# Order of uppers, loads and the first outer-product step in a retention + two-FFN kernel

## Chip, cores and metric

One core of a Trainium2 chip. The metric is device time in microseconds (us) of one execution. Besides it a profile gives the span, from the first to the last instruction that the profiler recorded.

## What is computed

Three stages, each fed by the one before; inputs are 32-bit floats, the weights arrive as 64-bit floats.

```
# q, k, v: (4, 8, 768, 64); gamma[h] = 1 - 2**(-5 - h); scale = 1/sqrt(64)
state = gamma * state + k[t] (outer) v[t]
y[t]  = scale * q[t] @ state
x = y as (3072 tokens, 512)
h = x @ w_in;  g = max(0.01*h, h);  x = g @ w_out        # 512x2048, 2048x512
h = x @ w2_in; g = h - tanh(h);     out = g @ w2_out
```

## The kernel before

**Attention (functions `a_*`).** 24 steps, one for each of six blocks of 128 positions (`c`) and four pairs of heads (`p`), in chunked form. A step on TensorE: transposes of the keys (`kTp`) and queries (`qTp`), the state's part of `y`, the scores' part of `y`, the state update `u` (not in the last block), and the next step's scores `sc`. ACT scales the keys two steps ahead (`k`) and copies the transposes to SBUF (`kT`, `qT`) and `y` to `x1`; DVE applies decay and mask to the scores (`A`) and updates the state `U`. All engines work in the order in which the program issues.

**Two parts for each matrix operand.** A 32-bit matrix is an upper part (a rounded copy, made by ACT in `upper`) and a lower part (the difference, made by DVE or POOL in `lower`); a product of two matrices takes three matmuls: upper by upper, upper by lower, lower by upper.

**Stream: the first GEMM of FFN1.** For three groups of blocks `sb` (two blocks `c` each) and eight groups `g` of columns of `w_in`, a 2x2 block product is made of seven products P1 to P7 (a Strassen-like scheme) in place of eight, six 128x512 matmuls each. Their results meet in PSUM banks X, Y and Z. `build_wg(g)` makes the operands of a weight set: the sums `s12` and `s34` on DVE, their uppers on ACT and lowers on DVE. `build_xc(sb, part)` makes the seven blocks of activations: B11, B21, T1 in part 0; T2, B22, T3, T4 in part 1. The T blocks are differences made in place by `minus` (T1, T2 on DVE; T3, T4 on POOL), then split into `xch` (upper) and `xcl` (lower). For sb 0 the blocks come from tiles in SBUF, later ones are loaded back by `load_xq`, which shares four buffers with the weights' loads. `stream` is the list of products, sorted by 56·sb + 7·g + an offset of each product (P1 0, P2 1, P5 2, P6 4, P3 5, P7 10, P4 13). After a product `collect` has ACT copy its bank (P1, P5, P6), or DVE add a kept copy to a bank (`add_up`, tile `c`), and one product later ACT rectifies `c` (`rectify`) and SP stores it to `g1s`.

**Background work.** Conversions of weights (`Convert`: ACT takes the absolute value, `cv<-raw`, DVE four steps), weight sets and blocks are generators. `run(queues, us)` takes steps from the first queue that has one ready until the time estimate `us` is used up; a generator that yields None is passed over. In the attention the queues are conversions (`conv`) and `bg`, taking turns as the first; in the stream `bg`, `bx` (loads and blocks), `conv`.

**Outer products and FFN2.** `mm_out1(n)`, n = 0 to 95, multiplies one `g` tile (split by `split_g` into `gh`, `gl`) with rows of `w_out`, 12 matmuls into four banks. FFN2 follows with `mm_l1` and `mm_l2`.

Of the kernel before, what the change touches and what calls it, by code (L numbers as in the profile page):

```python
# [19 lines left out]
P = 128  # L20
NB, NH, NS, ND = 4, 8, 768, 64
DM, DFF = 512, 2048
NC = NS // P
# [46 lines left out]
def kernel(  # L70
# [49 lines left out]
    def run(queues, us):  # L120

        while us > 0:
            for queue in queues:
                cost = next(queue[0], "end") if queue else None
                if cost is not None:
                    break
            if cost is None:
                return 0.0
            if cost == "end":
                queue.popleft()  # L130
            else:
                us -= cost
        return us

    def split(hi, lo, src, eng):

# [3 lines left out]
    def upper(hi, src, scale=None):  # L140
        if scale is None:
            nc.scalar.activation(out=hi, in_=src, func=AF.Copy)  # L142
        else:
            nc.scalar.activation(out=hi, in_=src, func=AF.Copy, scale=scale)
# [108 lines left out]
    def build_wg(g):  # L253
        while g + NG not in UN or g not in UN or len(free) < 10:
            yield None
        a, b = UN.pop(g), UN.pop(g + NG)
        s12, s34 = alloc("s12"), alloc("s34")
        w = {}
        ts = [alloc("wg", F32R) for _ in range(7)]
        for i, (n1, n2) in enumerate((("A11", "A12"), ("S1", "S2"), ("S3", "S4"))):  # L260
            hi, lo = ts[2 * i], ts[2 * i + 1]
            w[n1], w[n2] = (hi[:, :H2], lo[:, :H2]), (hi[:, H2:], lo[:, H2:])
        w["N22"] = ts[6][:, :H2], ts[6][:, H2:]
        upper(ts[0], a)
        nc.vector.tensor_tensor(out=s12[:, :H2], in0=b[:, :H2], in1=b[:, H2:], op=ALU.add)
        yield 0.4
        nc.vector.tensor_tensor(out=s12[:, H2:], in0=s12[:, :H2], in1=a[:, :H2], op=ALU.subtract)
        yield 0.4
        upper(ts[2], s12)
        lower(ts[0], ts[1], a)  # L270
        yield 0.7
        nc.vector.tensor_tensor(out=s34[:, :H2], in0=a[:, :H2], in1=b[:, :H2], op=ALU.subtract)
        yield 0.4
        nc.vector.tensor_tensor(out=s34[:, H2:], in0=a[:, H2:], in1=s12[:, H2:], op=ALU.subtract)
        yield 0.4
        upper(ts[4], s34)
        lower(ts[2], ts[3], s12)
        yield 0.7
        upper(w["N22"][0], b[:, H2:], -1.0)
        lower(ts[4], ts[5], s34)  # L280
        yield 0.7
        lower(*w["N22"], b[:, H2:], -1.0)
        give(a, s12, b, s34)
        WG[g] = w, ts
        yield 0.4
# [18 lines left out]
    def build_xc(sb, part, done=None):  # L304
        while sb not in XQ:
            yield None
        q = XQ[sb]
        old = SPAN * sb - 7
        b11, b12, b21, b22 = q["B11"], q["B12"], q["B21"], q["B22"]

        def minus(eng, out, x, y):
            for kt in range(2):
                eng.tensor_tensor(out=out[kt], in0=x[kt], in1=y[kt], op=ALU.subtract)  # L313


        todo = (("B11", b11, "P1", None), ("B21", b21, "P2", (nc.vector, b11, b12, b11)), ("T1", b11, "P5", None),
                ("T2", b11, "P6", None), ("B22", b22, "P3", (nc.gpsimd, b12, b22, b12)), ("T3", b12, "P7", None),
                ("T4", b21, "P4", None))
        for nm, src, by, nxt in todo[:3] if part == 0 else todo[3:]:
            while sb and now[0] < old + PROD[by][3]:  # L320
                yield None
            if sb:
                for t2 in XC[sb - 1].pop(nm):
                    give(*t2)
            while len(free) < 8:
                yield None
            if nm == "T2":
                minus(nc.vector, b11, b22, b11)
            out = [(alloc("xch", F32R), alloc("xcl", F32R)) for _ in range(2)]
            for kt in range(2):  # L330
                upper(out[kt][0], src[kt])
            yield 0.0
            for kt in range(2):
                lower(*out[kt], src[kt])
                yield 0.7
            XC.setdefault(sb, {})[nm] = out
            if nxt:
                minus(*nxt)
                yield 1.3 if nxt[0] is nc.vector else 0.0
            if nm == "T3":  # L340
                minus(nc.gpsimd, b21, b11, b21)
        if done:
            done()
# [221 lines left out]
    def load_g(n):  # L565
        if n < NT:
            GR[n] = alloc("gr")
            nc.sync.dma_start(out=GR[n], in_=g1s[n // NM, n % NM])


    stream = sorted((SPAN * sb + 7 * g + PROD[nm][3], sb, g, nm)
                    for sb in range(NSB) for g in range(NG) for nm in PROD)
# [63 lines left out]
    conv.extend((conversion(conv2[:W2_EARLY], made(1)),  # L636
                 conversion(conv_out, made(2))))
    bg.extend(build_wg(g) for g in range(2, NG))
    bx = deque()
    for sb in range(1, NSB):  # L640
        bx.extend((load_xq(sb, SPAN * (sb - 1) + 38), build_xc(sb, 0), build_xc(sb, 1)))
    xleft = [(c, p) for c in range(2, NC) for p in range(NPAIR)]
    us = 0.0
    for i, (at_, sb, g, nm) in enumerate(stream):
        an, bn, bk, _ = PROD[nm]
        while g not in WG or bn not in XC.get(sb, {}):
            tick[0] += 1
            run((bg, bx, conv), 0.01)
        product(sb, g, nm)
        now[0] = at_  # L650
        tick[0] += 1
        done, late[:] = late[:], []
        used = collect(sb, g, nm)
        for args in done:
            rectify(*args)
        if sb == NSB - 1 and nm == "P4":
            give(*WG[g][1])
        if xleft:
            c, p = xleft.pop(0)
            t = xw.pop((c, p))  # L660
            nc.sync.dma_start(out=x1s[c, p], in_=t)
            give(t)
        us = run((bg, bx, conv), min(us + SLOT_US - used, SLOT_US))
        if len(stream) - 8 <= i < len(stream) - 8 + G_AHEAD:
            load_g(i - len(stream) + 8)
    for args in late:
        rectify(*args)
    for t2 in XC[NSB - 1].values():
        for t in t2:
            give(*t)  # L670


    xk, xr = {}, {}
    G, H, ACC, Q = {}, {}, {}, {}

    def split_g(n, eng):
        if n < NT:
            G[n] = alloc("gh", F32R), alloc("gl", F32R)
            split(*G[n], GR[n], eng)
            give(GR.pop(n))  # L680

    def mm_out1(n):
        nb, m = divmod(n, NM)
        if m == 0:
            for j in range(4):
                ACC[j] = bank(nb % 2 * 4 + j, f"o1_{nb}_{j}")
        g, w = G.pop(n), WO[m]
        for j in range(4):
            c = slice(j * P, (j + 1) * P)
            for i, (a, b) in enumerate(((w[0][:, c], g[0]), (w[0][:, c], g[1]), (w[1][:, c], g[0]))):  # L690
                nc.tensor.matmul(ACC[j], a, b, start=m == 0 and i == 0, stop=m == NM - 1 and i == 2)  # L691
        give(*g)
        if nb == NC - 1:
            give(*WO.pop(m))
        if m == NM - 1:
            for j in range(4):
                st = alloc("st")
                nc.scalar.activation(out=st, in_=ACC[j], func=AF.Copy)
                nc.sync.dma_start(out=x2s[nb, j], in_=st)
                give(st)  # L700

    def load_x(nb):
        if nb < NC:
# [30 lines left out]

    def mm_l1(n):
        nb, m = divmod(n, NM)
        h = bank(n % 4, f"h_{n}")
        w = W2[m][0]
        for kt in range(NK):
            x = xk[nb, kt]  # L740
            c = slice(kt * P, (kt + 1) * P)
            for i, (a, b) in enumerate(((w[0][:, c], x[0]), (w[0][:, c], x[1]), (w[1][:, c], x[0]))):
                nc.tensor.matmul(h, a, b, start=kt == 0 and i == 0, stop=kt == NK - 1 and i == 2)  # L743
            if m == NM - 1:
                give(*x)
        H[n] = h

    def mm_l2(n):
        nb, m = divmod(n, NM)
        if m == 0:  # L750
            for j in range(4):
                ACC[j] = bank(4 + j, f"acc_{nb}_{j}")
        g, w = G.pop(n), W2[m][1]
        for j in range(4):
            c = slice(j * P, (j + 1) * P)
            for i, (a, b) in enumerate(((g[0][:, c], w[0]), (g[0][:, c], w[1]), (g[1][:, c], w[0]))):
                nc.tensor.matmul(ACC[j], a, b, start=m == 0 and i == 0, stop=m == NM - 1 and i == 2)  # L757
        give(*g)
# [32 lines left out]
        split(*G[n], gt, nc.gpsimd if n < NT - 1 else nc.vector)  # L791
        give(gt)

    for n in range(2):
        split_g(n, nc.vector)
    conv.append(conversion(conv2[W2_EARLY:]))
    bg = deque([second_weights()])
    us = 0.0
    first_x = None
    for n in range(NT):  # L800
        load_g(n + G_AHEAD)
        while n % NM not in WO:
            tick[0] += 1
            run((conv,), 0.01)
# [97 lines left out]
```

## Time and profile before

| | |
|---|---|
| median of 3 runs | 1156.65 us (1155.52 to 1158.4) |
| the profiled execution | 1157.96 us |
| its span | 1156.2 us, 16460 instructions |
| mean granted clock of TensorE | 0.996 |
| busy: TensorE, its weight loads | 1133.6 (98%), 935.9 (81%) us |
| busy: DVE, ACT, POOL | 755.2 (65%), 590.6 (51%), 187.2 (16%) us |

Time outside the span (1.8 us here) belongs to the execution but has no instruction. Busy shares are averages over stages: the attention ends and the stream begins at 127.20 us, the outer products begin at 366.09 us, the rest is FFN1's second GEMM and FFN2. The granted clock is 1 at 2.4 GHz and 0.5 at 1.2 GHz; a stretch that has both shows a value between.

### The profile page before, as it was taken

What the parts mean: (1) busy time and instruction counts of PE and PEld (TensorE: products, weight loads), DVE (VectorE), ACT (ScalarE), POOL (GpSimd) and SP (SyncE); (2) the same over time, 40 slices, a digit from 0 to 9 for tenths busy, and PEclk for the clock granted to TensorE, in tenths of its full rate; (3) what the DMA queues carried; (4) which work ended last, traced back from release to release, by engine and by line L of the source; (5) the groups of instructions that cost most, each with busy time, mean ns of one, the idle gap of its engine ahead of it and who ended that gap; (6) DMA issues with size and microseconds to landing.
All of it is one profiled execution on the core that took longest, in us unless ns stands there. A gap on an engine that the chain in (4) does not pass through costs nothing.

```text
span 1156.2 us, 16460 instructions
## 1 busy us (share of the span) xinstructions
PE 1133.6 (98%) x6075; PEld 935.9 (81%) x6075; DVE 755.2 (65%) x1252; ACT 590.6 (51%) x1025; POOL 187.2 (16%) x168
## 2 busy tenths in 40 slices
PE   9988999899998999999999999999999999999998
PEld 6877788688886888888888888888888888888886
DVE  3577885765677663662644667667767767767765
ACT  5765665655666342341553455455554555545543
POOL 3332000202000000000000232232232232232221
PEclk9999999999999999999999999999999999999999
DMA  9996274575668674773850100200200200200000
GB/s 230 253 234 166 112 253 173 177 242 192 219 219 294 224 260 170 289 276 118 326 219 31 70 1 1 73 1 1 73 1 1 73 1 1 73 1 1 37 1 37
DMA packets 134448, 148.02 MB, mean 128 GB/s; under 512 B 57440, under 2 KB 86240, under 8 KB 134368
## 3 DMA queue, kind: packets, MB, share of 16 engines
q1 hardware_dynamic: 134080, 146.83, 38.1%
q8 instruction: 47, 0.77, 0.3%
q14 instruction: 33, 0.27, 0.1%
q10 hardware_dynamic: 288, 0.15, 0.0%
HBM read 96.61 MB, written 50.33 MB: 127 GB/s over the span
## 4 chain that ended last, share of the span: by engine, by line
PE 79%; DVE 1%; ACT 1%; issue 1%; DMA 0%; SPq 0%; DVEq 0%; ACTq 0%
PE o L691 23%; PE acc L757 23%; PE h L743 23%; PE X L599 6%; PE Y L599 3%; PE Z L599 2%; DVE xcl L148 0%; ACT xch L142 0%; ACT c L588 0%; DMA raw<-in_moe_w_out_dram 0%; DVE c L612 0%; DVE xq_B L313 0%; ACT cv L176 0%; ACT P L606 0%; DVE cv L185 0%
## 5 line engine op out<-in xcount | busy, mean ns | idle before, releaser
L691 PE MATMUL o<-gh,wo 128*128 128x512 f32 x768 | 238.3, 391 | 2.3 <-ACT gh L137 2.3
L138 POOL TENSOR_TENSOR gl<-e,gh 128x512 fp32r<-128x512 f32 x95 | 122.9, 1295 | 703.8 <-ACT gh L137 644.2
L137 ACT ACTIVATE gh<-e 128x512 fp32r<-128x512 f32 x96 | 60.7, 633 | 220.0 <-DVE e L784 220.0
L691 PEld LDWEIGHTS o<-gh,wo 128*128 128x128 f32 x768 | 144.9, 189 | 32.8 <-ACT gh L137 2.8
L777 DVE SCALAR_TENSOR_TENSOR e<-e,h 128x512 f32<-128x512 f32 x96 | 66.0, 687 | 152.7 <-ACT e L775 152.7
L691 PE MATMUL o<-gl,wo 128*128 128x512 f32 x384 | 150.0, 391 | 0.2 <-DVE gl L138 0.2
L757 PE MATMUL acc<-w2h,gl 128*128 128x512 f32 x384 | 149.6, 390 | 0.0
L757 PE MATMUL acc<-w2h,gh 128*128 128x512 f32 x384 | 149.4, 389 | 0.0
L757 PE MATMUL acc<-w2l,gh 128*128 128x512 f32 x384 | 149.4, 389 | 0.0
L743 PE MATMUL h<-xkh,w2h 128*128 128x512 f32 x384 | 149.4, 389 | 0.0
L743 PE MATMUL h<-xkl,w2h 128*128 128x512 f32 x384 | 149.4, 389 | 0.0
L743 PE MATMUL h<-xkh,w2l 128*128 128x512 f32 x384 | 149.4, 389 | 0.0
L138 DVE TENSOR_TENSOR gl<-gr,gh 128x512 fp32r<-128x512 f32 x96 | 64.4, 686 | 105.7 <-ACT gh L137 104.0
L599 PE MATMUL X<-xch,wg 128*128 128x512 f32 x384 | 127.7, 392 | 1.5 <-DVE c L612 1.0
L599 PEld LDWEIGHTS X<-xch,wg 128*128 128x128 f32 x384 | 72.7, 189 | 17.8 <-DVE c L612 1.6
L691 PEld LDWEIGHTS o<-gl,wo 128*128 128x128 f32 x384 | 72.5, 189 | 15.8 <-DVE gl L138 0.5
L757 PEld LDWEIGHTS acc<-w2h,gl 128*128 128x128 f32 x384 | 72.0, 188 | 15.7 <-DVE gl L138 0.4
L743 PEld LDWEIGHTS h<-xkh,w2l 128*128 128x128 f32 x384 | 72.1, 188 | 15.1
L757 PEld LDWEIGHTS acc<-w2l,gh 128*128 128x128 f32 x384 | 72.1, 188 | 15.0
L743 PEld LDWEIGHTS h<-xkh,w2h 128*128 128x128 f32 x384 | 72.1, 188 | 15.0
L757 PEld LDWEIGHTS acc<-w2h,gh 128*128 128x128 f32 x384 | 72.0, 188 | 15.0 <-ACT gh L137 0.2
L743 PEld LDWEIGHTS h<-xkl,w2h 128*128 128x128 f32 x384 | 72.0, 187 | 14.9
(91 smaller groups left out, 1877.3 us busy)
## 6 DMA issues: line engine op xcount, KB each, us to landing
g1s<-c SPq DMA_DIRECT2D x96, 256.0 KB, 2.1
gr<-g1s SPq DMA_DIRECT2D x96, 256.0 KB, 4.8
raw<-in_moe_w_in_dram SPq DMA_DIRECT2D x32, 512.0 KB, 5.6
raw<-in_moe_w_out_dram SPq DMA_DIRECT2D x32, 512.0 KB, 4.4
w2s<-cv SPq DMA_DIRECT2D x32, 256.0 KB, 4.3
w2r<-w2s SPq DMA_DIRECT2D x16, 512.0 KB, 5.5
q<-in_q_dram SPq DMA_DIRECT2D x24, 256.0 KB, 3.7
k<-in_k_dram SPq DMA_DIRECT2D x48, 128.0 KB, 3.8
```

Of the source, the lines that this page charges most:

```text
L137: nc.scalar.activation(out=hi, in_=src, func=AF.Copy)
L138: eng.tensor_tensor(out=lo, in0=src, in1=hi.bitcast(F32), op=ALU.subtract)
L599: nc.tensor.matmul(ps, w[:, c], x, start=first and kt == 0 and i == 0, stop=kt == 1 and i == 2, skip_group_check=True)
L691: nc.tensor.matmul(ACC[j], a, b, start=m == 0 and i == 0, stop=m == NM - 1 and i == 2)
L743: nc.tensor.matmul(h, a, b, start=kt == 0 and i == 0, stop=kt == NK - 1 and i == 2)
L757: nc.tensor.matmul(ACC[j], a, b, start=m == 0 and i == 0, stop=m == NM - 1 and i == 2)
L777: nc.vector.scalar_tensor_tensor(out=w, in0=u, scalar=C3, in1=h, op0=ALU.mult, op1=ALU.mult)
```

## The change

Three edits; the number of instructions stays the same on every engine.

1. A generator `settle()` yields None until the program has moved on by a product or step. `build_wg` waits in it between each pair of sums and their upper part, `build_xc` for T1 and T2 of sb 0. T2's difference now has a cost (1.3) in the queue's account.
2. `load_xq` has a queue of its own, `loads`, which is asked first. In sb 0, at every second product, `conv` is asked ahead of `bg`.
3. `split_g(0)` and `split_g(1)` come behind the fourth and third products from the end, and `mm_out1(0)` stands between the last two. The outer products take the banks in swapped order, and so do `h` and `acc` of FFN2.

```diff
+    def settle():
+        t = tick[0]
+        while tick[0] == t:
+            yield None
...
         nc.vector.tensor_tensor(out=s12[:, H2:], in0=s12[:, :H2], in1=a[:, :H2], op=ALU.subtract)
         yield 0.4
+        yield from settle()
         upper(ts[2], s12)
...
         nc.vector.tensor_tensor(out=s34[:, H2:], in0=a[:, H2:], in1=s12[:, H2:], op=ALU.subtract)
         yield 0.4
+        yield from settle()
         upper(ts[4], s34)
...
             if nm == "T2":
                 minus(nc.vector, b11, b22, b11)
+                yield 1.3
+            if not sb and nm in ("T1", "T2"):
+                yield from settle()
...
-                ACC[j] = bank(nb % 2 * 4 + j, f"o1_{nb}_{j}")
+                ACC[j] = bank((nb + 1) % 2 * 4 + j, f"o1_{nb}_{j}")
...
-    bx = deque()
-    for sb in range(1, NSB):
-        bx.extend((load_xq(sb, SPAN * (sb - 1) + 38), build_xc(sb, 0), build_xc(sb, 1)))
+    bx = deque(build_xc(sb, part) for sb in range(1, NSB) for part in range(2))
+    loads = deque(load_xq(sb, SPAN * (sb - 1) + 38) for sb in range(1, NSB))
...
-            run((bg, bx, conv), 0.01)
+            run((loads, bg, bx, conv), 0.01)
...
-        us = run((bg, bx, conv), min(us + SLOT_US - used, SLOT_US))
+        us = run((loads, bg, bx, conv) if sb or at_ % 2 else (loads, conv, bg, bx), min(us + SLOT_US - used, SLOT_US))
         if len(stream) - 8 <= i < len(stream) - 8 + G_AHEAD:
             load_g(i - len(stream) + 8)
-    for args in late:
-        rectify(*args)
+        if len(stream) - 4 <= i < len(stream) - 2:
+            split_g(i - len(stream) + 4, nc.vector)
+        if i == len(stream) - 2:
+            mm_out1(0)
...
-    for n in range(2):
-        split_g(n, nc.vector)
...
         load_g(n + G_AHEAD)
+        if n == 0:
+            split_g(2, nc.vector)
+            continue
```

**In the attention, on ACT.** The stretch around the uppers of T1 (`xch<-x1_1`, `xch<-x1_3`); numbers in names count allocations, and lines differ between the two kernels (L142 and L148 are `upper`). Before:

```order
L498 ACTIVATE x1_22_907<-y_10_890 128x512
L142 ACTIVATE xch_23_935<-x1_1_201 128x512
L142 ACTIVATE xch_25_937<-x1_3_337 128x512
L416 ACTIVATE k_13_788<-k_13_788,lead_65 128x4x64 x2
L439 ACTIVATE kT_12_963<-kTp_12_958 128x512
```

After:

```order
L509 ACTIVATE x1_22_907<-y_10_890 128x512
L427 ACTIVATE k_13_788<-k_13_788,lead_65 128x4x64 x2
L450 ACTIVATE kT_12_958<-kTp_12_953 128x512
L463 ACTIVATE qT_12_883<-qTp_12_2_960 128x2x2x128
L509 ACTIVATE x1_23_983<-y_11_966 128x512
L182 ACTIVATE cv_24_1009<-raw_9_0_860 128x512
L427 ACTIVATE k_14_868<-k_14_868,lead_65 128x4x64 x2
L450 ACTIVATE kT_13_1028<-kTp_13_1023 128x512
L463 ACTIVATE qT_14_1030<-qTp_14_0_1031 128x2x2x128
L509 ACTIVATE x1_25_1054<-y_12_1037 128x512
L148 ACTIVATE xch_26_1080<-x1_1_201 128x512
L148 ACTIVATE xch_28_1082<-x1_3_337 128x512
```

The two uppers moved from behind `x1_22` to behind `x1_25`, two steps on. The sums of the two weight sets in the attention have their uppers moved in the same way.

**At the start of the stream, on ACT and DVE.** In the kernel before, the four uppers of T2 and B22 stand on ACT in the attention:

```order
L498 ACTIVATE x1_59_1654<-y_20_1637 128x512
L142 ACTIVATE xch_60_1683<-x1_1_201 128x512
L142 ACTIVATE xch_62_1685<-x1_3_337 128x512
L142 ACTIVATE xch_64_1691<-x1_6_538 128x512
L142 ACTIVATE xch_66_1693<-x1_8_673 128x512
L416 ACTIVATE k_23_1554<-k_23_1554,lead_65 128x4x64 x2
```

After the change they stand behind the first products' copies (`P1_65`, `P5_68`) and the rectification of `c_67`, ahead of the copy of P6 (ACT):

```order
L645 ACTIVATE P1_65_1831<-X_0_0_1824 128x512
L182 ACTIVATE cv_66_1836<-raw_5_0_1732 128x512
L645 ACTIVATE P5_68_1859<-Y_0_0_1852 128x512
L627 ACTIVATE c_67_1848<-c_67_1848 128x512
L148 ACTIVATE xch_69_1866<-x1_1_201 128x512
L148 ACTIVATE xch_71_1868<-x1_3_337 128x512
L148 ACTIVATE xch_73_1874<-x1_6_538 128x512
L148 ACTIVATE xch_75_1876<-x1_8_673 128x512
L645 ACTIVATE P6_77_1887<-X_0_0_1824 128x512
```

DVE after the change, from the last step's second `A` to the sum `c_67` and the first lower of T2 (L321 is `minus`, here T2's sum; `cv` steps are a conversion's):

```order
L487 SCALAR_TENSOR_TENSOR A_23_1_1786<-sc_23_1_1775,cst_100 128x512
L154 TENSOR_TENSOR wg_53_1541<-s12_48_1536,wg_52_1540 128x512
L154 TENSOR_TENSOR wg_55_1543<-s34_49_1537,wg_54_1542 128x512
L156 SCALAR_TENSOR_TENSOR wg_56_1544<-cv_24_1009,wg_56_1544 128x256
L321 TENSOR_TENSOR x1_1_201<-x1_6_538,x1_1_201 128x512
L321 TENSOR_TENSOR x1_3_337<-x1_8_673,x1_3_337 128x512
L191 SCALAR_TENSOR_TENSOR cv_59_1615<-raw_4_0_1464,cv_59_1615 128x512
L194 SCALAR_TENSOR_TENSOR cv_59_1615<-raw_4_0_1464,cv_59_1615 128x512
L186 TENSOR_SCALAR cv_62_1734<-cv_62_1734 128x512
L188 TENSOR_SCALAR cv_62_1734<-cv_62_1734 128x512
L191 SCALAR_TENSOR_TENSOR cv_62_1734<-raw_12_0_1613,cv_62_1734 128x512
L651 TENSOR_TENSOR c_67_1848<-Z_0_0_1841,P1_65_1831 128x512
```

Before, `c_78` (the first sum, of the same product) had four steps of one conversion and two lowers between itself and the last lower of B22.

**At the end of the stream, on TensorE.** Before, the six matmuls of the last product P4 (`X_2_7`) stand right ahead of the first outer-product step (`o1_0_0` to `o1_0_3`). After the change the end of that step, the product, and the beginning of the next step read:

```order
L598 MATMUL o1_0_3_4026<-gh_413_3988,wo_332_3462 128x512
L598 MATMUL o1_0_3_4026<-gl_414_3989,wo_332_3462 128x512
L598 MATMUL o1_0_3_4026<-gh_413_3988,wo_333_3463 128x512
L638 MATMUL X_2_7_3901<-xch_318_3363,wg_178_2405 128x512
L638 MATMUL X_2_7_3901<-xcl_319_3364,wg_178_2405 128x512
L638 MATMUL X_2_7_3901<-xch_318_3363,wg_178_2405 128x512
L638 MATMUL X_2_7_3901<-xch_320_3365,wg_178_2405 128x512
L638 MATMUL X_2_7_3901<-xcl_321_3366,wg_178_2405 128x512
L638 MATMUL X_2_7_3901<-xch_320_3365,wg_178_2405 128x512
L598 MATMUL o1_0_0_4023<-gh_416_4005,wo_338_3502 128x512
```

The twelve matmuls of step 0 moved ahead of P4. On DVE the sum `c` that frees P4's bank now stands behind two `gl`:

```order
L144 TENSOR_TENSOR gl_414_3989<-gr_401_3929,gh_413_3988 128x512
L191 SCALAR_TENSOR_TENSOR cv_400_3925<-raw_12_1_3860,cv_400_3925 128x512
L194 SCALAR_TENSOR_TENSOR cv_400_3925<-raw_12_1_3860,cv_400_3925 128x512
L144 TENSOR_TENSOR gl_417_4006<-gr_403_3944,gh_416_4005 128x512
L651 TENSOR_TENSOR c_418_4015<-X_2_7_3901,P5_402_3938 128x512
```

Before, the same `c` (`c_414`) stood directly behind the two conversion steps.

On SP the four loads of the second group of blocks stand five stores of `g1s` earlier than before.

## Rows read from the trace of the kernel before

**Rows 1.** The page, busy time of each engine, share of the span.

```profile
PE 1133.6 (98%) x6075; PEld 935.9 (81%) x6075; DVE 755.2 (65%) x1252; ACT 590.6 (51%) x1025; POOL 187.2 (16%) x168
```

**Rows 2.** What TensorE waits for: us in total, times, longest.

```profile
PE sc L472 <- ACT kT L439: 9.9, 7, 2.8
PE o L691 <- ACT gh L137: 2.3, 1, 2.3
PE Y L599 <- ACT xch L142: 2.1, 1, 2.1
...
PE X L599 <- DVE c L612: 1.0, 1, 1.0
```

**Rows 3.** The chain that ended last, one piece: start, us, what.

```profile
220.25 2.72 PE X L599 x12
```

**Rows 4.** Timeline of TensorE in the attention, scores of three steps.

```profile
53.28 1.16 PE L472 MATMUL sc<-qT,kT 64*128 64x128 f32 x16
...
57.91 1.16 PE L472 MATMUL sc<-qT,kT 64*128 64x128 f32 x16
...
123.65 1.16 PE L472 MATMUL sc<-qT,kT 64*128 64x128 f32 x16
```

**Rows 5.** Timeline of ACT, the uppers of T1 in the attention.

```profile
61.21 1.23 ACT L142 ACTIVATE xch<-x 128x512 fp32r<-128x512 f32 x2 [3.05 <-DVE x L313]
```

**Rows 6.** Timeline of TensorE in the stream and at its end.

```profile
127.20 0.50 PE L599 MATMUL X<-xch,wg 128*128 128x512 f32 x1
...
131.42 0.39 PE L599 MATMUL X<-xch,wg 128*128 128x512 f32 x1
...
203.27 0.39 PE L599 MATMUL Z<-xch,wg 128*128 128x512 f32 x1
...
214.32 0.40 PE L599 MATMUL Y<-xch,wg 128*128 128x512 f32 x1
...
288.75 0.50 PE L599 MATMUL X<-xch,wg 128*128 128x512 f32 x1 [0.51 <-ACT P L606]
...
363.38 0.40 PE L599 MATMUL X<-xch,wg 128*128 128x512 f32 x1
...
371.50 0.62 PE L691 MATMUL o<-gh,wo 128*128 128x512 f32 x2
```

**Rows 7.** Windows: stretch, us; busy us PE, PEld, DVE, ACT, POOL; PEclk, DMA, GB/s.

```profile
57.91:123.65 65.74, 56.09 (x817) 48.59 (x813) 50.22 (x84) 37.89 (x78) 18.11 (x22) 0.97 0.67 176
127.20:160.00 32.80, 32.80 (x146) 27.16 (x146) 28.82 (x56) 23.36 (x44) 0.00 (x0) 1.00 0.69 246
207.00:211.00 4.00, 4.00 (x11) 3.16 (x12) 3.91 (x5) 2.78 (x5) 2.82 (x2) 0.57 0.00 0
```

**Rows 8.** Timeline of SP, the loads of the second group of blocks.

```profile
190.34 1.96 SPq L296 DMA_DIRECT2D xq_B<-x1s  x4
```

**Rows 9.** Timeline of DVE, late attention and end of the stream.

```profile
113.16 0.41 DVE L150 SCALAR_TENSOR_TENSOR wg<-cv,wg 128x256 fp32r<-128x256 f32 x1
113.50 1.29 DVE L313 TENSOR_TENSOR x<-x,x 128x512 f32<-128x512 f32 x2
114.88 3.86 DVE L148 TENSOR_TENSOR xcl<-x,xch 128x512 fp32r<-128x512 f32 x3
...
120.52 0.42 DVE L180 TENSOR_SCALAR cv<-cv 128x512 f32<-128x512 f32 x1
...
121.43 0.69 DVE L185 SCALAR_TENSOR_TENSOR cv<-raw,cv 128x512 int32<-128x512 int32 x1
...
124.84 1.29 DVE L476 SCALAR_TENSOR_TENSOR A<-sc,cst 128x512 f32<-128x512 f32 x2 [0.59 <-PE sc L472]
...
361.37 0.68 DVE L612 TENSOR_TENSOR c<-X,P 128x512 f32<-128x512 f32 x1
...
366.07 1.90 DVE L138 TENSOR_TENSOR gl<-gr,gh 128x512 fp32r<-128x512 f32 x3 [2.38 <-ACT gh L137]
```

**Rows 10.** Timeline of POOL, T4's sum in the attention.

```profile
114.33 3.26 POOL L313 TENSOR_TENSOR x<-x,x 128x512 f32<-128x512 f32 x2 [17.02 <-DVE x L313]
```

More of the change, by code (lines that the diff above doesn't have):

```diff
@@ L568, in load_g, with split_g, mm_out1 @@
             nc.sync.dma_start(out=GR[n], in_=g1s[n // NM, n % NM])
+    G, ACC = {}, {}
+    def split_g(n, eng):
+        if n < NT:
+            G[n] = alloc("gh", F32R), alloc("gl", F32R)
+            split(*G[n], GR[n], eng)
+            give(GR.pop(n))
+    def mm_out1(n):
+        nb, m = divmod(n, NM)
+        if m == 0:
+            for j in range(4):
+                ACC[j] = bank((nb + 1) % 2 * 4 + j, f"o1_{nb}_{j}")
+        g, w = G.pop(n), WO[m]
+        for j in range(4):
+            c = slice(j * P, (j + 1) * P)
+            for i, (a, b) in enumerate(((w[0][:, c], g[0]), (w[0][:, c], g[1]), (w[1][:, c], g[0]))):
+                nc.tensor.matmul(ACC[j], a, b, start=m == 0 and i == 0, stop=m == NM - 1 and i == 2)
+        give(*g)
+        if nb == NC - 1:
+            give(*WO.pop(m))
+        if m == NM - 1:
+            for j in range(4):
+                st = alloc("st")
+                nc.scalar.activation(out=st, in_=ACC[j], func=AF.Copy)
+                nc.sync.dma_start(out=x2s[nb, j], in_=st)
+                give(st)
     stream = sorted((SPAN * sb + 7 * g + PROD[nm][3], sb, g, nm)
@@ L673 @@
     xk, xr = {}, {}
[L674 to L685, printed above, removed]
-                ACC[j] = bank(nb % 2 * 4 + j, f"o1_{nb}_{j}")
[L687 to L700, printed above, removed]
+    H, Q = {}, {}
     def load_x(nb):
@@ L736, in mm_l1 @@
         nb, m = divmod(n, NM)
-        h = bank(n % 4, f"h_{n}")
+        h = bank(4 + n % 4, f"h_{n}")
         w = W2[m][0]
@@ L751, in mm_l2 @@
             for j in range(4):
-                ACC[j] = bank(4 + j, f"acc_{nb}_{j}")
+                ACC[j] = bank(j, f"acc_{nb}_{j}")
         g, w = G.pop(n), W2[m][1]
```

## Prediction

> **What bounds the kernel now.** The page's busy times come first: TensorE works in 98% of the span [rows 1], so there is nothing to shorten but its waits and the stretches at its lower clock. The table of its waits [rows 2] shows where they lie: 9.9 us of score matmuls (`sc`) waiting for ACT's copy of the transposed keys (`kT`), all in the attention, and single waits of 2.1 us (`Y`, a product of the stream), 1.0 us (`X`) and 2.3 us (the first outer-product step, `o`). A wait of the table is not the whole loss, since a restart costs some tenths and the granted clock can fall behind it; so each loss is read from the timeline as time between two matmuls less the undisturbed pace. That pace is twelve 128x512 matmuls in 2.72 us, 0.227 us each [rows 3].
>
> **Attention, what is won.** One undisturbed step takes 57.91 − 53.28 = 4.63 us; the next twelve take 123.65 − 57.91 = 65.74 us instead of 55.56, so 10.2 us are lost [rows 4]. Three of the twelve have no state update and need less than 4.63, so 10.2 is a floor. The reason stands on ACT: the upper parts of T1 wait 3.05 us for the sum on DVE [rows 5], and the scaling of the next keys and `kT` are queued behind them. Seven such waits make the 9.9 us, six of them in these twelve steps: behind the sums of T1, of two weight sets with two pairs of sums each, and of T2. The change queues these uppers a step later (five places) or out of the attention (T2). By then the sum is done, and in the first listing ACT goes from `x1_22` straight to the next keys. I take 10.5 us as won; 3 us of it are left where DVE becomes late instead (below).
>
> **Start of the second group of blocks, 203 us.** From 203.27 to 214.32 TensorE does 24 matmuls [rows 6], which take 5.44 us undisturbed: 5.6 us lost, in the waits for `xch` and `xcl` and at a clock of 0.57 in 207 to 211 us [rows 7], between its levels of 1.2 and 2.4 GHz. The cause is the order: the loads of the blocks are issued at 190.34 us [rows 8], a few products ahead of their use, and T1's uppers then wait for its sum. With loads in a queue of their own the order puts them five stores earlier on SP, eight products in all, so that T1's uppers stand four products ahead of P5 instead of two. The stores behind the four loads leave later; nothing reads them before the outer products, 150 us on. I take the whole 5.6 us; if half stays, 2.8. At 288.75 [rows 6] P6 waits 0.51 us for the copy of P1, which is queued behind uppers that wait for a sum: with a restart 0.7 us, gone.
>
> **End of the stream.** The last product P4 waits 1.0 us for DVE's `c` [rows 2], and the 15 matmuls from 363.38 to 371.50 take 8.12 us instead of 3.40 [rows 6]: 4.7 us, together 5.7. After the change 12 matmuls (2.72 us) of step 0 lie between P7 and P4, from about 361.0 to 363.7. Two `gl` are now ahead of `c` on DVE (0.6 each), so `c`, which began at 361.37 [rows 9], begins at 362.6 and ends at 363.3, 0.4 us before P4 wants the bank. Step 1 has its operands by then. Step 2's `gh` stands behind two rectifications and a conversion on ACT, where I expect 0.3 us. Won: 5.4 us. If 0.4 us of cover is not there, P4 waits a part of 1.2 us. The swapped banks cost nothing: the same count of banks, and step 0 takes those of Y and Z, whose products are over.
>
> **Start of the stream, what is lost.** In the kernel before, T2 and B22 were split in the attention. Now their uppers come behind the rectification of `c_67` on ACT, right ahead of the copy of P6. P6 of group 0, the fourth product, needs the first of them; before, it began 131.42 − 127.20 = 4.22 us after the first product [rows 6]. When is `c_67` done? DVE's list behind the last `A` (which ended at 124.84 + 1.29 = 126.13, 1.07 us before the first product [rows 9]) is: two lowers and the two T2 sums with the 512-wide rows (1.29 a pair), one 256-wide lower (0.41), three of the conversion's two-input steps (0.69), two one-input steps (0.42), then `c_67` (0.68). That is 1.29 + 1.29 + 0.41 + 2.07 + 0.84 + 0.68 = 6.6 us, which ends 5.5 us after the first product. The first T2 sum also releases T4's sum on POOL. Before, that pair took 3.26 us [rows 10], and the three `xcl` beside it 3.86 us instead of the 1.90 of three such operations alone [rows 9]: 2.0 us more. The same neighbours meet here, so `c_67` ends at 7.5. Then its rectification and `xch_69` on ACT, 1.2 us as the pair in [rows 5]: P6 starts at about 8.7 instead of 4.2, a wait of 4.5 us. With `xcl_70` behind it (0.65 less what the first matmul covers: 0.5) and 0.2 for the restart (the first matmul after a wait has 0.50 us at 127.20, a later one 0.39) it is 5.2 us. Behind the wait of 2.1 us at 205 the clock fell, and 11 matmuls took 4.00 us instead of 2.49 [rows 7]; I add 1.5 for the same here. Lost: 6.7 us. Behind the waiting rectification stand all four uppers; P3, the next, has its own by 10.9, when P6 ends. The bounds are 0 (the copy and the uppers come in time) and 8.0 (below).
>
> The Trainium skill, page "SBUF — State Buffer", section "Who interferes with whom", says that a VectorE instruction with two inputs in SBUF contends with a GpSimd instruction that reads SBUF, and that whichever issues second is blocked fully. The rows agree that it costs; they show 2.0 us, not the full 3.26 of the pair. By the rule taken whole P6 would wait 1.3 us longer and the time be 1143.7 us; with no contention at all it would be 1140.4.
>
> **Weight sets in the stream.** With the pauses each set takes two more queue turns, and from 127.20 to 160 us DVE is busy 28.82 of 32.80 us [rows 7], 88%, so a set has little slack. In the order two sets (groups 2 and 3) have their first lowers directly ahead of the products P1 that use them. Each then waits for two lowers, 1.3 us, less what DVE is ahead: I take 0.75 and 0.55, together 1.3. The bounds are 0 and, for all six sets, 9.0 (below). The turns of conversions and sets change nothing in the sum by themselves: they are the same instructions.
>
> **The sum.** Won 10.5 + 5.6 + 0.7 + 5.4 = 22.2; lost 6.7 + 1.3 = 8.0; net 14.2 us. The profiled execution took 1157.96 us with a span of 1156.2; it would take 1143.8 with 1142.0. It was 1.3 us above the median of the runs, 1156.65, so the median becomes **1142.4 us**.
>
> **Rivals.**
> - *The new wait does not come.* DVE is through the list before P6 needs it. For it: the list is 6.6 us without its neighbours on POOL, and each instruction counts; DVE is busy 50.22 of 65.74 us in the attention [rows 7], so what stands ahead of the last `A` need not be late. Against it: the list stands behind that `A` in the order and ACT's uppers behind `c_67`, so it would have to shrink to 2 us. 1142.4 − 6.7 = 1135.7 us.
> - *DVE becomes the bound of the first eight groups.* Each of six sets stalls its P1 by about 1.5 us, clock included: 9.0 in place of 1.3, 1150.1 us. For it: the 88%. Against it: no P1 waits for a set before.
> - *The attention's waits come back under another name.* Shifted uppers meet a DVE that is late with `A`, and 3 us of 10.5 are won: 1149.9 us. For it: 50.22 us of DVE work would fill 91% of the shorter 55.2 us. Against it: T2's sums and lowers, some 5 us, leave this stretch, and no wait for `A` is among the large ones today.
> - *Both of the last two*: 1157.6 us, no change that can be measured.
> - *Slower.* A whole set, seven DVE instructions of about 0.6 us, stands between the product that asks for it and its P1 in each of groups 2 to 7; with their 4.2 us and a share of the clock's fall 4.5 us a group, 27 in all less 1.3: 1168 us. It decides from (1160.1 − 1142.4 + 1.3) / 6 = 3.2 us a group. Against it: in the order the last instructions of a set, not the first, stand nearest to its P1.
> - That the change does not do what it says can be left out: the listings show the uppers, loads and step moved.
>
> **How the numbers follow.** I give the forecast 0.60, the hidden wait 0.10, the bound on DVE 0.12, the attention's waits 0.10, both 0.05, slower 0.03. The forecast's own range is 1139 to 1147 us. Each of its terms has both bounds, and the attention and the wait of P6 alone move it by 7 us either way: the range is 1135 to 1151, which holds the hidden wait (1135.7), the bound on DVE (1150.1) and the attention's waits (1149.9). About 0.3%, 3.5 us, is what can be told from no change here: faster is below 1153.2 and has 0.60 + 0.10 + 0.12 + 0.10 = 0.92, the same 0.05, slower above 1160.1 0.03.
>
> **What would show it.** Right: no row of `sc` waiting for `kT` above some tenths, and twelve steps in about 55 us; one wait of P6 in group 0 for `xch` of about 4.5 us, 4 us behind the first product, with a granted clock below 0.7 behind it; no wait for `xch` at the start of the second group of blocks; P4 and the first outer-product steps without waits over 0.5 us. Wrong: `sc` or `y` waiting for `A` in the attention; rows of P1 waiting for `wg` in most groups; P6 starting on time; or a wait of P4 in front of the outer products. It would be wrong above all if the size of the P6 wait is not what the list on DVE says.

## The result, and the profile after

The changed kernel takes 1147.22 us at the median of four runs, beside 1157.53 for the kernel before: a ratio of 0.9912 (95% interval 0.989 to 0.9934), 10.3 us less by the medians. The forecast was 1142.4 us in a range of 1135 to 1151. The profiled execution takes 1147.07 us with a span of 1145.3, 10.9 us less than before; the forecast of the span was 14.2 less.

The page and the table of TensorE's waits, which answer to [rows 1, 2] (us in total, times, longest; three short rows left out):

```profile
PE 1131.6 (99%) x6075; PEld 933.7 (82%) x6075; DVE 754.2 (66%) x1252; ACT 592.6 (52%) x1025; POOL 188.4 (16%) x168
...
PE X L638 <- ACT xch L148: 4.0, 1, 4.0
PE X L638 <- ACT P L645: 3.0, 1, 3.0
PE wps L401 <- DVE warm L398: 1.2, 1, 1.2
PE X L638 <- DVE c L651: 0.5, 1, 0.5
```

All rows of [rows 2] are gone or below 0.6 us. Two new ones stand in their place: 4.0 us for `xch`, which was forecast, and 3.0 us for a copy `P`, which was not. The timeline of TensorE shows where, beside [rows 4, 6]:

```profile
57.91 1.16 PE L483 MATMUL sc<-qT,kT 64*128 64x128 f32 x16
...
103.22 1.16 PE L483 MATMUL sc<-qT,kT 64*128 64x128 f32 x16
...
107.38 1.16 PE L483 MATMUL sc<-qT,kT 64*128 64x128 f32 x16
...
111.57 1.16 PE L483 MATMUL sc<-qT,kT 64*128 64x128 f32 x16
115.12 0.50 PE L638 MATMUL X<-xch,wg 128*128 128x512 f32 x1
...
119.13 0.39 PE L638 MATMUL Y<-xch,wg 128*128 128x512 f32 x1
123.55 0.79 PE L638 MATMUL X<-xch,wg 128*128 128x512 f32 x1 [4.04 <-ACT xch L148]
124.28 0.79 PE L638 MATMUL X<-xcl,wg 128*128 128x512 f32 x1
...
130.32 0.39 PE L638 MATMUL X<-xcl,wg 128*128 128x512 f32 x1
...
182.67 0.39 PE L638 MATMUL X<-xch,wg 128*128 128x512 f32 x1
186.06 0.50 PE L638 MATMUL X<-xch,wg 128*128 128x512 f32 x1 [2.99 <-ACT P L645]
```

The twelve attention steps take 53.66 us instead of 65.74: 12.1 us won. Between the matmuls that start at 119.13 and 130.32 TensorE gets through seventeen in 11.19 us instead of 3.85: 7.3 us lost. A window of that stretch shows a granted clock of 0.50, which is 1.2 GHz, for all of it (columns as in [rows 7]):

```profile
123.50:129.60 6.10, 6.05 (x14) 4.45 (x15) 3.41 (x6) 3.20 (x7) 0.00 (x0) 0.50 0.79 259
```

DVE and POOL at the start of the stream, to be read beside [rows 9, 10]:

```profile
115.50 1.29 DVE L321 TENSOR_TENSOR x<-x,x 128x512 f32<-128x512 f32 x2
116.71 1.79 DVE L191 SCALAR_TENSOR_TENSOR cv<-raw,cv 128x512 int32<-128x512 int32 x1
118.53 1.66 DVE L194 SCALAR_TENSOR_TENSOR cv<-raw,cv 128x512 int32<-128x512 int32 x1
...
121.64 0.68 DVE L651 TENSOR_TENSOR c<-Z,P 128x512 f32<-128x512 f32 x1
```

```profile
116.33 3.31 POOL L321 TENSOR_TENSOR x<-x,x 128x512 f32<-128x512 f32 x2 [18.28 <-DVE x L321]
```

`c_67` ends at 122.32 (121.64 + 0.68), 7.2 us behind the first product; two conversion steps beside POOL's sum take 3.45 us together (1.79 + 1.66) instead of two times 0.69.

The second loss begins on SP and DVE. DVE stands still from 177.2 us on, about 6 us before TensorE has to wait at the P6 of that group (DVE, then SP, then ACT; the line on landing is of the view of the tile `g1s` from 160 to 205 us):

```profile
176.80 0.42 DVE L271 TENSOR_TENSOR s<-cv 128x256 f32<-128x256 f32 x1
184.11 0.69 DVE L651 TENSOR_TENSOR c<-Y,P 128x512 f32<-128x512 f32 x1 [6.90 <-DMA g1s<-c]
```

```profile
173.79 1.97 SPq L304 DMA_DIRECT2D xq_B<-x1s  x4
176.14 16.14 SPq L628 DMA_DIRECT2D g1s<-c  x6
```

```profile
184.89 0.63 ACT L627 ACTIVATE c<-c 128x512 f32<-128x512 f32 x1 [6.57 <-DVE c L651]
185.42 0.58 ACT L645 ACTIVATE P<-X 128x512 f32<-128x512 f32 x1
```

```profile
DMA to landing us min/median/max: 2.0/2.0/7.9
```

A sum `c` on DVE waits 6.9 us for the end of a store of `g1s`. In the program that sum (`c_179`) gets the buffer of `c_168` from the list of free buffers, eleven allocations later, and `c_168`'s store is the first behind the four loads on SP. Stores land in 2.0 us at the median; this one was issued at 176.14, and the longest landing in the view, 7.9 us, ends when DVE goes on. On ACT the rectification of the sum waits for it, and behind that stands the copy `P` that P6 waits for. TensorE loses 3.16 us at 186.06 and 0.9 around it, the wait for a later `c` at 189.58 included, 4.0 in all.

### The profile page after: what moved, and what is told of

Read it like the earlier page. It is cut to its first block, busy times and chain, and to the rows that moved or that the text cites. A ratio compares the mean times of both kernels' runs of the same rounds, so it can differ in the third digit from the quotient of the medians.

```text
span 1145.3 us, 16466 instructions
## 1 busy us (share of the span) xinstructions
PE 1131.6 (99%) x6075; PEld 933.7 (82%) x6075; DVE 754.2 (66%) x1252; ACT 592.6 (52%) x1025; POOL 188.4 (16%) x168
## 4 chain that ended last, share of the span: by engine, by line
PE 80%; DVE 2%; ACT 1%; issue 1%; DVEq 0%; ACTq 0%
PE acc L771 23%; PE h L757 23%; PE o L598 23%; PE X L638 7%; PE Y L638 3%; PE Z L638 2%; DVE xcl L154 1%; DVE c L651 0%; ACT c L627 0%; ACT xch L148 0%; DVE xq_B L321 0%; DVE gl L144 0%; DVE st L779 0%; ACT cv L182 0%; ACT gh L143 0%
```

## Experiments

Spans are of one profiled execution each, compared with the changed kernel's 1145.3 where nothing else is said; the executions of one kernel lie 1 to 7 us apart, so the readings rest on the waits in the traces and not on small differences of spans. Ratios are to the kernel before, run in turn on the same chip, with their 95% interval; the changed kernel's is 0.9912.

**Loads four products later.**

```diff
-    loads = deque(load_xq(sb, SPAN * (sb - 1) + 38) for sb in range(1, NSB))
+    loads = deque(load_xq(sb, SPAN * (sb - 1) + 42) for sb in range(1, NSB))
```

> The changed kernel with one number changed: the loads of the next blocks may start four products later (42 instead of 38 in the list of products), behind the store of the first sum c whose buffer is reused soonest, and still ahead of their use. Theory A (the 2 MB of loads stand ahead of that store on one DMA queue, the store lands 6 us late, and DVE's next c waits for its buffer): DVE's wait of 6.9 us for a store of g1s is gone, P6 of that group starts without its 3.0 us, and the span falls by 3.5 to 4.2 us from 1145.3, to about 1141.4, the median to about 1143.3. Rival B (buffers are short at this place because conversions and weight sets took turns, whatever the loads do): the wait stays at 3 us or more, span 1145. Rival C (the loads come too late for T1): the wait for xch at the next group of blocks comes back, 2 us or more, span 1145 to 1147.

Span 1141.7, median 1144.05, ratio 0.9876 (0.9857 to 0.9896): the span is 3.6 us less, the median 3.2. DVE's wait for a store falls to 1.0 us:

```profile
DVE c L651 <- DMA g1s<-c: 1.0, 1, 1.0
```

TensorE no longer waits at that P6, but loses 1.2 us at 195 us for a later `c`. Theory A holds; B and C are out. A store still takes 7.1 us to land here; what has changed is that nobody wants its buffer at once (DVE waits 1.0 us for a store, ACT 1.8).

**Loads on ACT's queue.**

```diff
-            nc.sync.dma_start(out=t, in_=x1s[2 * sb + th, ...])
+            nc.scalar.dma_start(out=t, in_=x1s[2 * sb + th, ...])
```

> The changed kernel with the loads of the next blocks issued on the DMA queue of ACT instead of SP's, at the same place. Theory A (the store waits because it stands behind the loads in its queue's order): the store lands in less than 4 us, DVE's wait falls from 6.9 to under 3 us, and the span falls by 3 to 4 us, less what ACT spends on issuing. Rival D (the store waits because the loads fill the DMA engines, whichever queue they come from): DVE's wait stays at 5 us or more, span 1144.5 to 1146.

Span 1143.1, median 1145.87, ratio 0.9891 (0.9871 to 0.991). DVE's wait:

```profile
181.72 0.69 DVE L651 TENSOR_TENSOR c<-Y,P 128x512 f32<-128x512 f32 x1 [5.50 <-DMA g1s<-c]
```

It stays at 5.5 us, as rival D has it, and the longest store takes 6.5 us. The loads were issued 2.5 us sooner (from 171.3 instead of 173.8), and DVE goes on 2.4 us sooner. The profiled span lies below D's 1144.5 to 1146; the other three executions had 1144.1 to 1144.7. So the store does not wait for its place in one queue alone: on SP's queue it is late behind loads on ACT's, and the loads delay it while they are in transfer. The Trainium skill, page "DMA: Bandwidth & Descriptors", section "Issuing engines are not separate DMA queues", says that transfers run on the same 16 engines whichever engine starts them; the 5.5 us agree with it.

**Loads in two pairs.** The second pair three products behind the first.

```diff
+            if nm == "B21":
+                half = tick[0] + 3
+                while tick[0] < half:
+                    yield None
```

> The changed kernel with the four loads of the next blocks in two pairs: B11 and B21 at the same place as now, B12 and B22 three products later. The store of the first c then stands behind 1 MB instead of 2 MB. Theory A (the store lands when the loads ahead of it have landed, and DVE's next c waits for that): DVE's wait falls from 6.9 us by the 3 to 3.5 us that the second MB takes, to 3.5 us or less, and P6's wait from 3.0 to under 0.5 us; a second, smaller wait may stand behind the second pair. Span 1142 to 1143.5. Rival B (the wait is set by something else at that place): the wait stays at 6 us or more, span 1145.

One run: 1144.02 us, span 1142.2.

```profile
DVE c L655 <- DMA g1s<-c: 4.3, 1, 4.3
```

The wait shrank by 2.6 us with half of the loads behind the store, a little less than expected, and TensorE's wait at P6 from 3.0 to 0.4 us; the longest store took 5.2 us. With the two runs above: the wait is set by what is in transfer ahead of the store, and by when its buffer is wanted.

**T2's uppers at once.**

```diff
-                yield 1.3
-            if not sb and nm in ("T1", "T2"):
+                yield 1.3 if sb else 0.0
+            if not sb and nm == "T1":
```

> The changed kernel without the wait of a step between T2's sum and its uppers, and with that sum's cost left out of the queue's account: the two uppers stand on ACT directly behind the last attention steps, ahead of the copy of P1, the sum c_67 and its rectification. Theory A (P6 waits because the moved uppers stand behind the rectification): P6 of group 0 starts within 0.5 us of its turn, and the span falls by 5 to 7 us, to about 1139. Rival B (DVE's list is what is late, with or without the place of the uppers): P6 starts in time but its second half waits for the lower xcl, which stands behind the conversion steps that slow beside POOL; 3 to 4.5 us stay lost, and the span falls by only 1 to 3 us.

Span 1144.8, median 1146.49, ratio 0.9904 (0.9877 to 0.9931): a span 0.5 us less, which cannot be told from none. P6 starts in time and then waits 4.0 us for its lower part, which stands behind the slow steps and `c_71` on DVE:

```profile
119.25 0.39 PE L638 MATMUL X<-xch,wg 128*128 128x512 f32 x1
119.47 0.39 PE L638 MATMUL X<-xcl,wg 128*128 128x512 f32 x1
119.70 0.61 PE L638 MATMUL X<-xch,wg 128*128 128x512 f32 x2
124.33 0.80 PE L638 MATMUL X<-xcl,wg 128*128 128x512 f32 x1 [4.02 <-DVE xcl L154]
```

Rival B holds in its mechanism: the place of the uppers on ACT is not the cause, DVE's list is. Its gain of 1 to 3 us hardly came. P6 and the products behind it lose 5.8 us here instead of 7.3, but the wait for the store grew (DVE 7.6 us, TensorE 3.7), the clock fell to 0.50 behind it, and that place costs 5.6 us instead of 4.0. Beside POOL's sum stood a lower (1.61 us) and one conversion step (1.78 us) in this run, and again they took about 2.0 us more than alone.

**T4's sum on DVE.**

```diff
-                minus(nc.gpsimd, b21, b11, b21)
+                minus(nc.gpsimd if sb else nc.vector, b21, b11, b21)
```

> The changed kernel with T4's sum of the first group of blocks on DVE instead of POOL, in the order of the program (later). Theory A (the sum on POOL costs its DVE neighbours 2.1 us): the two conversion steps that took 1.79 and 1.66 us take about 0.69 each, c_67 ends about 2.1 us earlier, the wait of P6 falls from 4.0 to about 1.9 us, and the span by 2.1 us or a little more where the clock falls less. DVE pays 1.3 us for the sum later, in a stretch with room. Rival B (the two slow steps are slow for another reason, such as the landing of their input): they stay at 1.7 us, the wait stays at 4 us, and the span stays at 1145 or rises by the 1.3 us.

Span 1142.4, median 1144.71, ratio 0.9883 (0.9863 to 0.9903).

```profile
117.01 0.68 DVE L191 SCALAR_TENSOR_TENSOR cv<-raw,cv 128x512 int32<-128x512 int32 x1
117.73 0.69 DVE L194 SCALAR_TENSOR_TENSOR cv<-raw,cv 128x512 int32<-128x512 int32 x1
...
119.86 0.68 DVE L651 TENSOR_TENSOR c<-Z,P 128x512 f32<-128x512 f32 x1
```

```profile
121.78 0.50 PE L638 MATMUL X<-xch,wg 128*128 128x512 f32 x1 [1.98 <-ACT xch L148]
```

The two steps take 0.68 and 0.69 us, and the wait of P6 is 2.0 instead of 4.0. The clock did not fall here, so this place costs 2.8 us instead of 7.3. The span gained only 2.9, since TensorE's wait for the store grew from 3.0 to 3.5 us and the clock fell behind that one: 5.4 us are lost there instead of 4.0. Theory A holds. The Trainium skill's rule on the shared reads (page "SBUF — State Buffer", section "Who interferes with whom") names the right pair of instructions; taken for the whole of POOL's pair, as the prediction also priced it, it asks too much: the two steps lost 2.07 us beside 3.31 us of POOL, so DVE was not shut out for all of it.

**The third edit alone,** on the kernel before.

> The kernel before with the third edit alone (two splits of g earlier, step 0 of the outer products between the last two products, banks swapped); nothing else moves. Theory A (the 5.7 us at the end of the stream are won whatever stands ahead): P4 of the last group and step 0 start without a wait, 0.3 us is left at the second matmul of step 2, the span falls from 1156.2 by 5.3 to 5.7 us, to about 1150.7, the median to about 1152. Rival B (the wait at the end had already been shortened by the other edits, so the third alone leaves a part): 2 us or more is left in front of P4 or step 1, span 1152.5 to 1154.

Median 1152.48, ratio 0.9952 (0.9937 to 0.9967), span 1149.3. At the end of the stream no wait is left but 0.3 us at step 2 (in the changed kernel too, 0.3). Theory A; the ratio is worth 5.6 us, and the further 1.2 us of the profiled span lie ahead of that place, where the edit moves nothing. The waits of the attention stay:

```profile
PE sc L478 <- ACT kT L445: 9.0, 7, 2.8
```

**The second edit alone,** on the kernel before.

> The kernel before with the second edit alone (loads in a queue of their own, turns of conversions and weight sets in the first eight groups). Theory A (the edit wins the 5.6 us at the second group of blocks but lets the loads meet the stores, in this order two copies and sums that reuse the buffers of stores behind the loads): no wait for xch at that place, 5 to 6 us won there, and a new wait of DVE or ACT for a store of g1s, with 1 to 4 us lost by TensorE; the seven waits of the attention stay. Span 1151.5 to 1154.5. Rival B (the new wait comes with the moved uppers and weight sets only): no wait for a store over 1 us, span about 1150.5.

Median 1152.1, ratio 0.9963 (0.9947 to 0.9979), span 1150.0. The wait for `xch` at 205 us is gone, the waits of the attention stay, and an operation of ACT waits for a store:

```profile
PE sc L472 <- ACT kT L439: 10.1, 7, 2.8
...
ACT P L606 <- DMA g1s<-c: 3.3, 1, 3.3
```

TensorE loses nothing by that wait, which ends at 190.83: it goes on at its undisturbed pace from 186.11 to 206.29. The 0.8 us that it does lose at 207.22 have another cause. The copy `P` that it waits for stands on ACT behind two uppers that wait for a sum (TensorE, then ACT):

```profile
207.22 0.50 PE L599 MATMUL X<-xch,wg 128*128 128x512 f32 x1 [0.55 <-ACT P L606]
```

```profile
203.41 1.24 ACT L142 ACTIVATE xch<-xq_B 128x512 fp32r<-128x512 f32 x2 [2.48 <-DVE xq_B L313]
```

So a wait for a store comes with this edit, as A says, but not the 1 to 4 us that A wanted TensorE to lose. Its price is set by which buffers are due and what stands behind them; with the other two edits it was 4.0. By the ratios the whole gains 10.2 us, the third edit 5.6 and the second 4.3, each uncertain by about 2 us. The 0.3 us that is left is not the worth of the first edit alone, which no run has: it also holds what the edits cost each other, the 4.0 us at the store among it.

**No turns of conversions and weight sets.**

```diff
-        us = run((loads, bg, bx, conv) if sb or at_ % 2 else (loads, conv, bg, bx), ...)
+        us = run((loads, bg, bx, conv), ...)
```

> The changed kernel without the turns of conversions and weight sets in the first eight groups (weight sets always first). By the order T2's uppers then stand ahead of the rectification of c_67, and the loads of the next blocks come five products later, behind the two stores whose buffers are reused soonest. Theory A (the loads' early place comes from the turns; DVE's list is what P6 waits for): DVE has no wait for a store of g1s over 1 us; P6 of group 0 starts in time, but its second matmul waits about 3.3 us for xcl, which stands behind c_67; the span falls by 3.5 to 5 us from 1145.3, to about 1141. Rival B (the turns are worth what they cost, since conversions or weight sets come late without them): new waits of P1 for wg in several groups, or of T1 for its loads, 3 us or more in all; span 1143.5 or more.

Median 1145.5, ratio 0.9892 (0.9877 to 0.9906), the profiled span 1145.4, the longest of four (the others 1142.2 to 1144.3).

```profile
124.02 0.50 PE L638 MATMUL X<-xcl,wg 128*128 128x512 f32 x1 [3.20 <-DVE xcl L154]
...
197.29 0.79 PE L638 MATMUL X<-xch,wg 128*128 128x512 f32 x1 [3.59 <-DVE c L651]
```

```profile
192.34 1.29 DVE L154 TENSOR_TENSOR xcl<-xq_B,xch 128x512 fp32r<-128x512 f32 x2 [4.82 <-DMA g1s<-c]
```

The first row is as expected. Against the expectation the wait for a store was not gone: with the loads later, DVE met it at another buffer, that of a lower part (`xcl`, third row); TensorE lost 3.8 us at 197.29, and the 12 matmuls from 197.88 on took 0.43 us each instead of 0.227. No P1 waits for `wg` and nothing waits for the loads of the blocks, so rival B's reason is out too. Turns or none, the time is the same within the runs' spread: the intervals of the two ratios overlap.

**Later loads and T4's sum on DVE together,** two runs of one kernel.

> The changed kernel with both edits that helped: the loads may start four products later (42 instead of 38), and T4's sum of the first group of blocks is on DVE. Theory A (the two losses are independent; where the P6 wait was cut, the clock did not fall): the P6 wait is 2.0 us and costs 2.8 in all instead of 7.6, and the wait of 3 to 3.5 us for the store's buffer is 1 us or less; the span falls by 8 to 9 us from 1145.3, to about 1137, the median to about 1139. Rival B (one gain takes from the other): the span stays above 1139.

> The kernel with later loads and T4's sum on DVE once more, for the clock behind the wait of 2.0 us of P6 in group 0: it stayed at 2.4 GHz in the kernel with T4's sum on DVE alone, and fell in this one. Theory A (it differs from one execution to the next): the twelve matmuls behind the wait can take 2.7 us this time, and the span is then about 1137.7. Rival B (the order of this kernel sets it): they take about 4.3 us again, span about 1139.4.

Median 1140.78, ratio 0.9852 (0.9837 to 0.9867), span 1139.4; the second time 1140.59 with a span of 1138.8. Windows over P6 and the products behind it, of the first and of the second execution:

```profile
121.00:127.50 6.50, 5.78 (x17) 4.37 (x18) 4.30 (x7) 3.64 (x7) 0.00 (x0) 0.74 0.75 245
```

```profile
121.00:127.50 6.50, 5.22 (x22) 4.07 (x23) 5.01 (x9) 4.70 (x10) 0.00 (x0) 1.00 0.73 244
```

The wait is 2.0 us in both; the clock fell in one (1.6 us lost) and not in the other, so theory A of the second run holds. The 8 to 9 us of the first expectation did not come: the single gains were 3.6 and 2.9 us, and together they gave 5.9 and 6.5. A wait for a later `c` stays, which costs TensorE 0.9 to 1.0 us. Neither gain took from the other, so rival B's reason does not hold either, though its span does. The second span fell by less than the clock gave, in part since its attention ended 0.5 us later.

**T2 ahead of the conversions,** on top of the two edits of the run above.

```diff
-        us = run((...) if sb or at_ % 2 else (loads, conv, bg, bx), ...)
+        us = run((...) if sb or at_ % 2 or at_ < 7 else (loads, conv, bg, bx), ...)
```

> As the kernel with later loads and T4's sum on DVE, and in the first seven places of the list of products weight sets and blocks come ahead of conversions, so that T2's uppers stand ahead of the rectification of c_67. Theory A (what is left of the P6 wait is DVE's list up to c_67): P6 of group 0 starts in time, its second matmul waits about 1.2 us for xcl, and the place costs 1.5 us instead of 2.8; span about 1135.7. Rival B (the conversion steps that now come later make a weight set late): a new wait of 1 us or more at P1 of groups 1 to 4, span 1137 or more.

Median 1139.43, ratio 0.9841 (0.9824 to 0.9857), span 1137.6. P6 starts in time and waits 1.2 us for `xcl` as expected, but P1 now waits for `wg` in two groups:

```profile
133.87 0.73 PE L638 MATMUL X<-xch,wg 128*128 128x512 f32 x2 [0.24 <-DVE wg L154]
...
144.08 0.74 PE L638 MATMUL X<-xch,wg 128*128 128x512 f32 x2 [0.40 <-DVE wg L154]
```

The two places cost about 0.5 and 0.7 us with their restarts: both theories hold in part.

**T2's pause ends with the first product,** on top of the run above.

```diff
                 minus(nc.vector, b11, b22, b11)
+                t = tick[0]
                 yield 1.3
-            if not sb and nm in ("T1", "T2"):
+                while not sb and tick[0] == t:
+                    yield None
+            if not sb and nm == "T1":
```

> As the kernel with T2 ahead of the conversions, and T2's pause ends with the first product (it counts from the sum, not from the end of the sum's cost), so that T2's two lowers stand ahead of c_67 and of four conversion steps on DVE. Theory A (what is left of the wait in P6 is DVE's list): the 1.2 us wait for xcl and its restart are gone, 1.4 us less than 1137.6: span about 1136.2, median about 1138. Rival B (conversions put off make weight sets late): the waits of P1 for wg in groups 2 and 3 grow from 0.4 and 0.6 us by 1 us or more, span 1137.5 or more.

Median 1138.19, ratio 0.9832 (0.9812 to 0.9852), span 1136.9: the fastest here, 9 us under the changed kernel by medians. P6 of group 0 has no wait at all, and instead two products at 148 and 152 us wait about 1 us each. On ACT (second view) a conversion's first step waits 3.0 us for its load, with an upper part of a weight set, its lower on DVE and the copy `P` behind it:

```profile
147.88 0.50 PE L641 MATMUL X<-xch,wg 128*128 128x512 f32 x1 [0.94 <-ACT P L648]
...
152.01 0.50 PE L641 MATMUL X<-xch,wg 128*128 128x512 f32 x1 [1.12 <-DVE c L654]
```

```profile
145.86 0.66 ACT L182 ACTIVATE cv<-raw 128x512 f32<-128x512 f32 x1 [3.03 <-DMA raw<-in_moe_w_in_dram]
146.43 0.61 ACT L148 ACTIVATE wg<-s 128x512 fp32r<-128x512 f32 x1
146.94 0.40 ACT L150 ACTIVATE wg<-cv 128x256 fp32r<-128x256 f32 x1
147.25 0.58 ACT L648 ACTIVATE P<-X 128x512 f32<-128x512 f32 x1
```

Theory A holds for P6, but the span fell by 0.7 us instead of 1.4; in the place of rival B's waits for `wg` stand these two, which have a late load at their head.

## Why the prediction was right, and where it was not

- **Attention: right, too small.** 12.1 us won against 10.5. The three steps without a state update take 4.16 us (107.38 − 103.22 in the timeline after), 0.47 less than 4.63, and the step behind them, which has no transposes of the queries, takes 4.19 (111.57 − 107.38); with these four the floor of 10.2 becomes 12.0. The prediction named three of them and priced 0.3 us. The seven waits for `kT` stay in both runs without the first edit (9.0 and 10.1 us), so neither of the other two edits removes them. The rival that the waits return as waits for `A` is out.
- **P6 of group 0: right, with its mechanism.** Forecast: `c_67` ends 7.5 us and P6 starts 8.7 us after the first product, a wait of 4.5. Measured: 7.2, 8.4 and 4.0. DVE's list took 6.2 us without POOL's share, forecast 6.6. POOL's share was 2.0 in the forecast and 2.07 in the trace, on two conversion steps in place of three lowers, and putting the sum on DVE took it away. The fall of the clock was mis-sized, 1.5 against 2.6 us; together 7.3 against 6.7. The upper bound of 8.0 us held, but the prediction gives no working for it. The rival that the wait does not come is out. The prediction has the uppers stand behind the rectification on ACT; the run with the uppers moved shows that DVE's list alone is enough.
- **Second group of blocks: right.** 5.6 us forecast; 0.7 us of small waits is left, some 4.9 won. The 0.7 us at the start of the third group hardly came: 0.6 us of other waits stands there now.
- **End of the stream: right.** 5.4 us forecast, and 0.3 us left at step 2, as forecast.
- **Weight sets: too large.** 1.3 us forecast; one wait of 0.35 us at 139.64. DVE as the bound of the first groups is out.
- **The step that failed** is the sentence on the earlier loads: "The stores behind the four loads leave later; nothing reads them before the outer products". Nothing reads what they store, but the next tile in the same buffer has to wait until the store has ended. Eleven allocations later a `c` had that buffer; DVE waited 6.9 us and TensorE lost 4.0, which the sum had at nothing. Moving the loads or splitting them made this wait shorter, and giving them another queue did not take it away; it alone accounts for more than the difference between 14.2 and 10.9.

In sums of the span: 12.1 + 4.9 + 0.1 + 5.4 − 7.3 − 0.4 − 4.0 = 10.8, against 10.9 measured. The attention and the weight sets came out 2.5 us better than forecast, which hid a part of the 4.0 us; nothing ties these terms to the store, so that much of the nearness is luck. Without it the median would have been near 1149.7, still inside the range.

The slower side never came near: its threshold was 3.2 us a group, and the one late weight set cost 0.35.

## What to carry to other kernels

When a large load is moved earlier, look at what shares the DMA engines with it, and for each store among them at who gets its buffer next: a store costs nothing only until its buffer is wanted again. When an operation is put off by a step to spare one engine, count the list of the engine that makes its input; moving the upper parts forward on ACT was worth little here, since a lower part was still late on DVE. A small sum on POOL can cost DVE more than doing the sum on DVE: here 2.07 us beside POOL, and 1.28 us for the sum itself.

## What the runs showed of the hardware that was not expected

The same kernel at the same place, behind the same wait of 2.0 us, ran its next matmuls at 2.4 GHz in one execution and partly at 1.2 GHz in another (granted clock 1.00 and 0.74 in the windows above). Waits of 3.2 to 3.7 us were followed by a fall in three kernels, the wait of 3.0 us at 186.06 was not. The fall behind the 2.0 us was worth 1.6 us, 0.14% of the span, so the span of a single execution does not settle a difference of 2 us here. What decides between the two levels behind a wait of this length is not shown.
